# The last output block in two PSUM banks, the wq/wk weights in eight transfers and one cast, and another layout of the bf16 values tile

## The chip, the cores and the metric

The kernel runs on one core of one Trainium2 chip. The metric is the device time of one execution in microseconds (us); smaller is better. The engines are called by the profile's names: PE (TensorE; PEld is its weight load), DVE (VectorE), ACT (ScalarE), POOL (GpSimd), and SP, which issues most of the transfers.

## What is computed

Sigmoid attention over 8 sequences of 448 tokens with 12 heads of 64, followed by a token-mixing MLP. The names are the reference's, cut to what matters:

```python
# q, k, v: (8, 12, 448, 64) float32
scores = q @ k^T / sqrt(64) - log(448)
attn = 1 / (1 + exp(-scores))
x = (attn @ v)                       # laid out as (8, 448, 768)
wq, wk = x @ w_q, x @ w_k            # (768 x 64 weights)
W_tok = wq @ wk^T / sqrt(64)         # (8, 448, 448)
out = relu(W_tok @ x) @ w_out        # (8, 448, 768) float32
```

## The kernel before

**Units of work.** Four heads of one sequence make a quad; there are 24 (three per sequence), numbered 0 to 23. For each quad seven score tiles are computed: `scores` (L298) fills two PSUM banks with four 64x64-tiled matmuls, and ACT turns them into a bf16 tile with one sigmoid over 128x896 (L303). There are 168 of those. `values` (L320) multiplies them with the quad's v and sums over the seven tiles. The MLP of a sequence follows in pieces (`mlp_wqk`, `mlp_tmp`, `mlp_mix`), and the last matrix product goes out in blocks of 384 columns (`out_pair` L509, `out_halves` L549, `out_chunk` L590). The order of all this on the engines is written out by hand: the string `PLAN` has a letter for each step, and the string `BANKS` names the bank or pair of banks that each step takes, in order, of the eight.

**Loads and casts.** Each quad needs q, k and v, 448 KB each in float32. The list `ORDER` gives the order of loading and casting; a name such as k5 is k of quad 5, and w0 stands for the two weight matrices wq and wk together (`load_weights`, L624; later w entries are pieces of wout). It begins:

```python
"W2 q1 k1 k2 q2 v0 k3 q3 v1 q4 k4 v2 w0 k5 q5 w1 v3 v4 .w6 k6 q6 w4 v5 q7 k7 v6 ..."
```

Before it stand q0 and k0, the latter in two parts (L645 to L647). All loads are issued by SP into eight buffers; `pump_loads` issues a load when the entry eight places ahead of it has been cast (`ring[-8] not in cast`), and w0 counts as one entry. The casts to bf16 run on POOL in the order of the list, all but a few that the list marks for DVE: `cast1` for q and k (L192 in one layout, L202 in another) and for v (L202), `cast_now` for w0 (L720). L630 is an issue of wout's load on POOL's own queue, which stands between the casts of q5 and v3.

The program gives the transfers of SP and ACT eight completion semaphores in rotation, and a transfer waits, ahead of its own issue, until the one eight places before it has landed. Counted from the first, q0 is transfer 1, k0 2 and 3, q1 4, k1 5, k2 6, q2 7, v0 8, k3 9, q3 10, v1 11, q4 12, k4 13, v2 14, wq 15, wk 16, k5 17, q5 18.

**wq and wk.** Two transfers put them side by side in one float32 buffer, 128 rows at a time (L624); four POOL casts of 64x384 then write `wqk16` in the order in which the matmuls take the rows, moving half of them to the other 64 partitions (L720).

**The end.** The last sequence pair ends in eight blocks of `out_chunk` on single banks, six 128x128-by-384 matmuls each (L590), in two steps of three. DVE or ACT copies a block to SBUF (L614). The last block is copied by both at once: DVE takes columns 384 to 575 (L611) and ACT columns 576 to 767 (L612). Both read one bank, and the program orders the second reader behind the first. The store (L599) goes in two halves of 64 partitions, one issued by SP and one by ACT.

Of the kernel before, what the change touches and what calls it, by code (L numbers as in the profile page):

```python
# [10 lines left out]
BF16 = mybir.dt.bfloat16  # L11
# [6 lines left out]
def kernel(  # L18
# [29 lines left out]
    def pool(name, bufs, **kw):  # L48
# [4 lines left out]
    p_c16 = pool("c16", 2)  # L53
    p_v16 = pool("v16", 4)
# [24 lines left out]
    )  # L79
    BANKS = BANKS.split()[::-1]  # L80

# [65 lines left out]
    ld = {}  # L147
# [39 lines left out]
    def cast1(n, nm, e):  # L187
        if KIND[n] in "cer" and nm != "v":
            if n not in pq:
                pq[n] = p_c16.tile([P, 2, 2, NI, 32, 2], BF16, tag="qk16", name="qk16")  # L190
            f = pq[n]
            COPY[e](  # L192
                out=f[:, :, "qk".index(nm)].rearrange("p e i d y -> p e y i d"),
                in_=ld.pop((nm, n)).rearrange("p (y i e d) -> p e y i d", y=2, i=NI, e=2),
            )
            ld[nm + "16", n] = f
            if ("q16", n) in ld and ("k16", n) in ld:
                arrange(n, nc.gpsimd)
            return
        p = p_v16 if nm == "v" else p_c16  # L200
        t16 = p.tile([P, NI, 2, HD], BF16, tag=nm + "16", name=nm + "16")
        COPY[e](  # L202
            out=t16.rearrange("p i b d -> p b i d"),
            in_=ld.pop((nm, n)).rearrange("p b (i d) -> p b i d", i=NI),
        )
        ld[nm + "16", n] = t16

    qk = {}
# [104 lines left out]
    def values(n, i, tail, eng):  # L313
        u, j = quads[n]
        if i == 0:
            pv[n] = bank2()
        fb, ps, _ = pv[n]
        for h in range(2):
            for g in range(2):
                nc.tensor.matmul(  # L320
                    ps[HALF[g], h, 0:S], ld["v16", n][HALF[h], i, g, :],
                    ats[n, i][HALF[h], g, :], start=(i == 0), stop=(i == NI - 1),
                )
        if i == NI - 1:
            if tail:
                for h in range(2):
                    read(fb, COPY["vs"[h]](out=xt(u, j)[:, h, 0:S], in_=ps[:, h, 0:S]))
            else:
                read(fb, COPY[eng](out=xt(u, j)[:, :, 0:S], in_=ps[:, :, 0:S]))  # L329
# [158 lines left out]
    chunks = []  # L488
    ot = {}

    opened = []
# [80 lines left out]
    def out_chunk(act, tail):  # L572

        if opened:
            w, m, nb, fb, ps = opened.pop()
            part = 1
        else:
            w, m, nb = chunks.pop(0)
            if nb < 0:
                nb = 0  # L580
                chunks.insert(0, (w, m, 1))
            fb, ps, _ = bank1()
            part = 0
        if nb == 0 and not part:
            ot[0] = p_o.tile([P, D], F32, tag="o", name="o")
        o = ot[0]

        def block(ps, w0, w1, c0, c1):
            for c in range(c0, c1):
                nc.tensor.matmul(  # L590
                    ps, mxs[w][:, 2 * S * c + m * P : 2 * S * c + (m + 1) * P],
                    wout16[:, c, w0:w1], start=(c == 0), stop=(c == NC - 1),
                )

        def store(cols):
            for y in range(2):
                b, i = divmod(2 * m + y, NI)
                eng = nc.scalar if tail and y else nc.sync
                eng.dma_start(  # L599
                    out=out[2 * w + b].rearrange("(p i) d -> p i d", i=NI)[:, i, cols],  # L600
                    in_=o[HALF[y], cols],
                )

        ps = ps[:, 0:NB] if not part else ps
        block(ps, nb * NB, (nb + 1) * NB, part * NC // 2, (part + 1) * NC // 2)
        if not part:
            opened.append((w, m, nb, fb, ps))
            return
        if w == NU // 2 - 1 and not chunks:
            h = NB // 2  # L610
            read(fb, nc.vector.tensor_copy(out=o[:, NB : NB + h], in_=ps[:, 0:h]), keep=True)  # L611
            read(fb, nc.scalar.copy(out=o[:, NB + h :], in_=ps[:, h:]), keep=True)  # L612
        else:
            read(fb, COPY["s" if act else "v"](out=o[:, nb * NB : (nb + 1) * NB], in_=ps), keep=True)  # L614
        split = tail and w == NU // 2 - 1 and m == NI - 1
        if nb or split:
            store(slice(nb * NB, (nb + 1) * NB) if split else slice(0, D))

    w32 = {}

    def load_weights():
        w32["qk"] = p_ld.tile([P, 2 * NI * HD], F32, tag="ld", name="w32")[:, 0:D]
        for x, w in enumerate((moe_w_q, moe_w_k)):
            nc.sync.dma_start(  # L624
                out=w32["qk"].rearrange("p (c n) -> p c n", c=NC)[:, :, 64 * x : 64 * x + 64],
                in_=w.rearrange("(c p) n -> p c n", p=P)
            )

    def load_wout(c):
        nc.gpsimd.dma_start(  # L630
# [11 lines left out]
    def cols(r):  # L642
# [9 lines left out]
        out=ident, in_=ident, compare_op=ALU.not_equal, fill=1.0, base=0,  # L652
# [22 lines left out]
        elif x[0].isupper():  # L675
            BY["s"].append((x[0].lower(), int(x[1:])))
    OTHERS = set(BY["s"] + BY["v"])
    ORDER = [(x[0], int(x[1:])) for x in ORDER.replace(".", "").lower().split()]
    done = dict.fromkeys("SPqkKxWNUMOCgz", 0)
    used, loaded, cast = set(), set(), set()  # L680

# [2 lines left out]
    def pump_loads():  # L684
        while len(loaded) < len(ORDER):
            nm, n = ORDER[len(loaded)]
            if nm == "w" and n:
                loaded.add((nm, n))
                continue
            if len(ring) >= 8 and ring[-8] not in cast:  # L690
                break
            ring.append((nm, n))
            if nm == "w":
                load_weights()
            else:
                load1(n, nm, nc.sync)
            loaded.add((nm, n))
# [13 lines left out]
    def cast_now(nm, n, e):  # L711
        if nm != "w":
            cast1(n, nm, e)
        elif n:
            if n % 3 == 1:
                load_wout(n - 1)
        else:
            for h in range(2):
                for g in range(2):
                    COPY[e](  # L720
                        out=wqk16[HALF[g], h::2],
                        in_=w32["qk"].rearrange("p (c n) -> p c n", c=NC)[HALF[h], g::2],
                    )
        cast.add((nm, n))
        pump_loads()

# [2 lines left out]
    def pump():  # L729
        while pumped[0] < len(ORDER):  # L730
            nm, n = ORDER[pumped[0]]
            if (nm, n) not in OTHERS:
                if not ready(nm, n):
                    break
                cast_now(nm, n, "g")
            pumped[0] += 1

    def cast_next(e):
# [7 lines left out]
    for t16, t32, r, e in ((q016, q0, IA, "v"), (q016, q0, IB, "s"), (k016, k0, KA, "g"), (k016, k0, KB, "g")):  # L746
        COPY[e](
            out=t16[:, r].rearrange("p i b d -> p b i d"),
            in_=t32[:, :, cols(r)].rearrange("p b (i d) -> p b i d", d=HD),
# [119 lines left out]
```

## Time and profile before

| what | us |
|---|---|
| median of 3 runs | 183.09 |
| lowest and highest of them | 182.22, 185.05 |
| the profiled execution, as timed | 182.05 |
| span of its profile | 180.3 |

| engine | busy us | instructions |
|---|---|---|
| PE | 169.6 | 3471 |
| ACT | 160.0 | 212 |
| DVE | 142.1 | 229 |
| POOL | 123.4 | 168 |

The span runs from the first to the last instruction of the profiled execution; what the timed figure has above it (1.8 us) lies around it. Times in the profile's rows count from the span's start. A row of the timeline has the start, the length and, in brackets, the idle time of its engine just before it with what ended that. DMA issues (SPq, ACTq) don't count as busy time of their engine.

### The profile page before, as it was taken

The numbers are of one execution on the slowest core, as the hardware profiler recorded it, in microseconds if no ns is written. First come the engines' busy times: TensorE is split into PE (matmuls) and PEld (weight loads), VectorE is DVE, ScalarE is ACT, GpSimd is POOL, SyncE is SP. The second block draws the span as 40 slices with busy tenths as digits, with TensorE's granted clock in tenths as the row PEclk, the third lists the DMA queues.
The fourth block names the chain that finished last, engine by engine and source line by source line (L and its number), as shares of the span: only waits on it lengthen the run. The fifth ranks groups of instructions, "written<-read, shape, count | busy, mean of one in ns | idle before, by whom it ended". The sixth has DMA issues, their size and how long they took to land.

```text
span 180.3 us, 7970 instructions
## 1 busy us (share of the span) xinstructions
PE 169.6 (94%) x3471; PEld 112.5 (62%) x3472; DVE 142.1 (79%) x229; ACT 160.0 (89%) x212; POOL 123.4 (68%) x168
## 2 busy tenths in 40 slices
PE   7787899889999999999999999999999999999990
PEld 7333555554455445655686768778987789778560
DVE  3239599998989899889899879887999866588810
ACT  4699999999999999999999989999999899985240
POOL 1397799998998999999999999989306990000000
PEclk9999999999999999999999999999999999999998
DMA  5999999999999799989998999983946744442686
GB/s 174 356 394 387 331 382 376 288 302 364 411 340 346 181 306 292 372 285 288 313 282 285 281 374 346 316 266 96 264 118 155 226 95 107 91 91 46 157 241 175
DMA packets 24915, 47.31 MB, mean 262 GB/s; under 512 B 3888, under 2 KB 18480, under 8 KB 24880
## 3 DMA queue, kind: packets, MB, share of 16 engines
q1 hardware_dynamic: 23680, 44.84, 77.0%
q0 software_dynamic: 800, 1.18, 3.6%
q10 hardware_dynamic: 400, 0.79, 1.4%
q8 instruction: 27, 0.44, 1.0%
q14 instruction: 8, 0.07, 0.1%
HBM read 35.78 MB, written 11.01 MB: 260 GB/s over the span
## 4 chain that ended last, share of the span: by engine, by line
PE 67%; DVE 14%; DMA 9%; POOL 4%; SPq 2%; ACT 2%; issue 2%
PE banks L298 13%; PE banks L320 13%; PE banks L590 13%; PE banks L509 11%; DVE qk L232 4%; DMA k<-in_k_dram 4%; DMA v<-in_v_dram 3%; PE banks L549 3%; PE banks L395 3%; DVE xt L329 3%; POOL qk L192 3%; PE banks L358 2%; DVE qk L256 2%; DVE xn L347 1%; DMA out_dram<-o 1%
## 5 line engine op out<-in xcount | busy, mean ns | idle before, releaser
L303 ACT ACTIVATE at<-banks 128x896 bf16<-128x896 f32 x168 | 140.9, 946 | 3.6 <-PE banks L298 2.7
L298 PE MATMUL banks<-qk 64*64 64x448 bf16 x672 | 62.5, 357 | 2.5 <-DVE xt L329 1.4
L320 PE MATMUL banks<-at,v 64*64 64x448 bf16 x672 | 46.5, 350 | 0.1
L298 PEld LDWEIGHTS <-qk 64*64 64x64 bf16 x672 | 25.8, 105 | 21.1 <-issue 12.5
L509 PE MATMUL banks<-wout,mx 64*64 64x384 bf16 x672 | 36.3, 323 | 0.0
L320 PEld LDWEIGHTS <-v 64*64 64x64 bf16 x672 | 23.7, 106 | 6.9 <-issue 0.8
L509 PEld LDWEIGHTS <-mx 64*64 64x64 bf16 x672 | 23.3, 107 | 4.3
L590 PE MATMUL banks<-wout,mx 128*128 128x384 bf16 x132 | 24.8, 327 | 0.0
L192 POOL CAST qk<-q 128x896 bf16<-128x896 f32 x19 | 22.6, 1191 | 0.7 <-DMA q<-in_q_dram 0.2
L450 DVE TENSOR_SCALAR mx<-banks 128x512 bf16<-128x512 f32 (+3 forms) x24 | 21.0, 882 | 2.4 <-PE banks L477 1.6
L161 POOL COPY swap<-qk 32x448 uint32<-32x448 uint32 x28 | 15.8, 564 | 10.2 <-DVE qk L192 8.5
L192 POOL CAST qk<-k 128x896 bf16<-128x896 f32 x18 | 21.5, 1194 | 1.8 <-POOL qk L167 0.9
L329 DVE CAST xt<-banks 128x896 bf16<-128x896 f32 x19 | 20.5, 1081 | 1.4 <-PE banks L320 1.0
L202 POOL CAST v<-v 128x896 bf16<-128x896 f32 x20 | 18.4, 931 | 0.6
L590 PEld LDWEIGHTS <-mx 128*128 128x128 bf16 x132 | 11.9, 98 | 10.7 <-issue 3.9
L164 POOL COPY qk<-qk 32x448 uint32<-32x448 uint32 x28 | 16.6, 592 | 1.6
L263 DVE STREAM_TRANSPOSE qk<-qk 128x448 f32<-128x448 f32 x28 | 17.3, 630 | 0.1
L167 POOL COPY qk<-swap 32x448 uint32<-32x448 uint32 x28 | 15.8, 564 | 1.6
L232 DVE STREAM_TRANSPOSE qk<-qk 32x448 f32<-32x448 f32 x24 | 15.3, 636 | 0.6
L371 DVE COPY xn<-banks 128x1024 bf16<-128x1024 bf16 (+1 forms) x17 | 11.1, 654 | 4.6 <-PE banks L358 4.6
L614 DVE COPY o<-banks 128x384 f32<-128x384 f32 x15 | 8.2, 550 | 1.6 <-PE banks L590 0.8
L358 PEld LDWEIGHTS <-xt 64*64 64x64 bf16 x544 | 7.6, 109 | 1.9 <-issue 1.0
(87 smaller groups left out, 196.2 us busy)
## 6 DMA issues: line engine op xcount, KB each, us to landing
q<-in_q_dram SPq DMA_DIRECT2D x24, 448.0 KB, 7.0
v<-in_v_dram SPq DMA_DIRECT2D x24, 448.0 KB, 6.3
k<-in_k_dram SPq DMA_DIRECT2D x23, 448.0 KB, 7.3
out_dram<-o SPq DMA_DIRECT2D x51, 192.0 KB, 3.5
wout<-in_moe_w_out_dram POOLq DMA_DIRECT2D x2, 576.0 KB, 12.1
wout<-wout SPq DMA_DIRECT2D x12, 96.0 KB, 5.2
out_dram<-o ACTq DMA_DIRECT2D x3, 192.0 KB, 3.4
k<-in_k_dram SPq DMA_DIRECT2D x1, 256.0 KB, 5.2
```

The lines of the kernel that those rows point to most:

```text
L164: eng.tensor_copy(out=w[hi, 0], in_=w[lo, 1])
L192: COPY[e](out=f[:, :, "qk".index(nm)].rearrange("p e i d y -> p e y i d"), in_=ld.pop((nm, n)).rearrange("p (y i e d) -> p e y i d", y=2, ...
L202: COPY[e](out=t16.rearrange("p i b d -> p b i d"), in_=ld.pop((nm, n)).rearrange("p b (i d) -> p b i d", i=NI),)
L232: nc.vector.transpose(out=qk[n][other : other + 32, h].rearrange("p t i n -> p (t i n)").bitcast(F32), in_=w[own : own + 32, 1 - h],)
L263: nc.vector.transpose(out=qk[n][:, t].rearrange("p t i n -> p (t i n)").bitcast(F32), in_=w)
L298: nc.tensor.matmul(sc[HALF[h], g, 0:S], qk[n][HALF[g], h, 1, i, :], qk[n][HALF[g], h, 0].rearrange("p i n -> p (i n)"), start=True, stop=True,
L303: inst = nc.scalar.activation(at, sc[:, :, 0:S], ACTF.Sigmoid, bias=attn_bias, scale=attn_scale)
L320: nc.tensor.matmul(ps[HALF[g], h, 0:S], ld["v16", n][HALF[h], i, g, :], ats[n, i][HALF[h], g, :], start=(i == 0), stop=(i == NI - 1),)
L329: read(fb, COPY[eng](out=xt(u, j)[:, :, 0:S], in_=ps[:, :, 0:S]))
L450: inst = nc.vector.tensor_scalar(dst, ps, moe_scale, 0.0, ALU.mult, ALU.max)
L509: nc.tensor.matmul(ps[HALF[x], y, 0:NB], mx[HALF[y], u, b, 64 * (i - 3 * y) : 64 * (i - 3 * y) + 64], wout16[HALF[y], slot(y, b), x * NB : ...
L590: nc.tensor.matmul(ps, mxs[w][:, 2 * S * c + m * P : 2 * S * c + (m + 1) * P], wout16[:, c, w0:w1], start=(c == 0), stop=(c == NC - 1),)
```

## The change

1. **Last output block.** The three-matmul steps of the block become two blocks of 192 columns, six matmuls each, in two banks. DVE copies the first, ACT the second, and the store follows. The block takes one bank more, so `BANKS` gets one entry more, bank 0. From the 97th entry on the names are exchanged, 0 with 2 and 1 with 3 (01 with 23); no entry is added, removed or moved before the last.
2. **wq and wk.** Eight transfers of 64 partitions and 48 KB each (two matrices, two halves of partitions, two of the interleaved row groups) put the rows straight into the order and the partitions in which they are needed, and one POOL cast of 128x768 takes the place of four of 64x384.
3. **Layout of v.** The bf16 tile of v is [2, 7, 64] per partition instead of [7, 2, 64], so that its cast writes 896 elements in one run instead of runs of 64. The matmuls of `values` read 64 neighbouring elements as before.
4. A mark `*` in `ORDER` would send a v cast to a DMA. `ORDER` has no such mark, so nothing takes that way.

`PLAN` and `ORDER` are not changed.

```diff
-        "45 01 67 45 01 2 3 4 5 6 7 0 1 "
+        "45 23 67 45 23 0 1 4 5 6 7 2 3 0 "
...
-        p = p_v16 if nm == "v" else p_c16
-        t16 = p.tile([P, NI, 2, HD], BF16, tag=nm + "16", name=nm + "16")
+        if nm == "v":
+            t16 = p_v16.tile([P, 2, NI, HD], BF16, tag="v16", name="v16")
...
+                COPY[e](
+                    out=t16.rearrange("p b i d -> p (b i d)"), in_=ld.pop((nm, n)).rearrange("p b x -> p (b x)"),
+                )
+            ld["v16", n] = t16
+            return
+        t16 = p_c16.tile([P, NI, 2, HD], BF16, tag=nm + "16", name=nm + "16")
...
-                    ps[HALF[g], h, 0:S], ld["v16", n][HALF[h], i, g, :],
+                    ps[HALF[g], h, 0:S], ld["v16", n][HALF[h], g, i, :],
...
+        if nb and w == NU // 2 - 1 and not chunks:
+
+            if part:
+                fb, ps, _ = bank1()
+            h = NB // 2
+            c0 = NB + part * h
+            block(ps[:, 0:h], c0, c0 + h, 0, NC)
+            read(fb, COPY["vs"[part]](out=o[:, c0 : c0 + h], in_=ps[:, 0:h]), keep=True)
+            if part:
+                store(slice(NB, D))
+            else:
+                opened.append((w, m, nb, fb, ps))
+            return
...
-        if w == NU // 2 - 1 and not chunks:
-            h = NB // 2
-            read(fb, nc.vector.tensor_copy(out=o[:, NB : NB + h], in_=ps[:, 0:h]), keep=True)
-            read(fb, nc.scalar.copy(out=o[:, NB + h :], in_=ps[:, h:]), keep=True)
-        else:
-            read(fb, COPY["s" if act else "v"](out=o[:, nb * NB : (nb + 1) * NB], in_=ps), keep=True)
+        read(fb, COPY["s" if act else "v"](out=o[:, nb * NB : (nb + 1) * NB], in_=ps), keep=True)
...
         for x, w in enumerate((moe_w_q, moe_w_k)):
-            nc.sync.dma_start(
-                out=w32["qk"].rearrange("p (c n) -> p c n", c=NC)[:, :, 64 * x : 64 * x + 64],
-                in_=w.rearrange("(c p) n -> p c n", p=P)
-            )
+            for g in range(2):
+                for h in range(2):
+                    nc.sync.dma_start(
+                        out=w32["qk"][HALF[g]].rearrange("p (j h n) -> p h j n", j=NJ, h=2)[:, h, :, 64 * x : 64 * x + 64],
+                        in_=w.rearrange("(j g h d) n -> g h d j n", j=NJ, g=2, h=2)[g, h],
+                    )
...
-            for h in range(2):
-                for g in range(2):
-                    COPY[e](
-                        out=wqk16[HALF[g], h::2],
-                        in_=w32["qk"].rearrange("p (c n) -> p c n", c=NC)[HALF[h], g::2],
-                    )
+            COPY[e](out=wqk16.rearrange("p c n -> p (c n)"), in_=w32["qk"])
```

More of the change, by code (lines that the diff above doesn't have):

```diff
@@ L199, in cast1 @@
             return
-        p = p_v16 if nm == "v" else p_c16
-        t16 = p.tile([P, NI, 2, HD], BF16, tag=nm + "16", name=nm + "16")
+        if nm == "v":
+            t16 = p_v16.tile([P, 2, NI, HD], BF16, tag="v16", name="v16")
+            if e == "d":
+                u, j = quads[n]
+                nc.gpsimd.dma_start(
+                    out=t16.rearrange("p b i d -> p b (i d)"),
+                    in_=v[u, 4 * j : 4 * j + 4].rearrange("(g h) (p i) d -> (h p) g (i d)", g=2, i=NI),
+                )
[6 more added lines that the diff above has]
+        t16 = p_c16.tile([P, NI, 2, HD], BF16, tag=nm + "16", name=nm + "16")
         COPY[e](
@@ L602, in store @@
                 )
+        if nb and w == NU // 2 - 1 and not chunks:
[7 more added lines that the diff above has]
+                store(slice(NB, D))
+            else:
+                opened.append((w, m, nb, fb, ps))
+            return
         ps = ps[:, 0:NB] if not part else ps
@@ L623, in load_weights @@
         for x, w in enumerate((moe_w_q, moe_w_k)):
-            nc.sync.dma_start(
-                out=w32["qk"].rearrange("p (c n) -> p c n", c=NC)[:, :, 64 * x : 64 * x + 64],
-                in_=w.rearrange("(c p) n -> p c n", p=P)
-            )
+            for g in range(2):
[3 more added lines that the diff above has]
+                        in_=w.rearrange("(j g h d) n -> g h d j n", j=NJ, g=2, h=2)[g, h],
+                    )
     def load_wout(c):
@@ L677 @@
     OTHERS = set(BY["s"] + BY["v"])
-    ORDER = [(x[0], int(x[1:])) for x in ORDER.replace(".", "").lower().split()]
+    CASTING = {("v", int(x[2:])) for x in ORDER.split() if x[0] == "*"}
+    ORDER = [(x[0], int(x[1:])) for x in ORDER.replace(".", "").replace("*", "").lower().split()]
     done = dict.fromkeys("SPqkKxWNUMOCgz", 0)
@@ L686, in pump_loads @@
             nm, n = ORDER[len(loaded)]
-            if nm == "w" and n:
+            if nm == "w" and n or (nm, n) in CASTING:
                 loaded.add((nm, n))
@@ L734, in pump @@
                     break
-                cast_now(nm, n, "g")
+                cast_now(nm, n, "d" if (nm, n) in CASTING else "g")
             pumped[0] += 1
```

14 rows, old and new, of the table BANKS are left out of this document.

## The prediction

> **What bounds the kernel now.** I read the page first: span, busy shares in slices, chain of waits.
>
> ```profile
> span 180.3 us, 7970 instructions
> ACT  4699999999999999999999989999999899985240
> PE 67%; DVE 14%; DMA 9%; POOL 4%; SPq 2%; ACT 2%; issue 2%
> ```
>
> PE holds most of the chain that ended last, but ACT is full (8 or 9 tenths) from the third slice to the 35th. The timelines of ACT and of the tail say where each rules (start, length, what).
>
> ```profile
> 8.59 51.65 ACT L303 ACTIVATE at<-banks 128x896 bf16<-128x896 f32 x63 [0.38 <-PE banks L298]
> 157.41 0.92 ACT L303 ACTIVATE at<-banks 128x896 bf16<-128x896 f32 x1
> 168.14 7.97 PE L590 MATMUL banks<-wout,mx 128*128 128x384 bf16 x48
> ```
>
> From 8.59 to 60.24 ACT runs 63 sigmoids without a gap, 0.82 us each. In this stage the time is ACT's: work saved on POOL, DVE or SP shortens nothing, and a delay there costs only what is left when the work already ahead of ACT has run out. After the last sigmoid (158.3) PE works off the rest; its last 48 matmuls end at 176.11, and the last copies, the last store and its landing follow in line. So the change has two places: the tail, where every tenth is paid out, and 13 to 30 us, where loads and casts either keep ahead or don't.
>
> **The tail.** The last rows of the same timeline:
>
> ```profile
> 175.38 0.48 ACT L614 COPY o<-banks 128x384 f32<-128x384 f32 x1 [0.70 <-DMA out_dram<-o]
> 175.89 0.50 ACTq L599 DMA_DIRECT2D out_dram<-o  x1
> 176.15 0.36 DVE L611 COPY o<-banks 128x192 f32<-128x192 f32 x1 [4.05 <-PE banks L590]
> 176.54 0.32 ACT L612 COPY o<-banks 128x192 f32<-128x192 f32 x1 [0.69 <-DVE o L611]
> 176.89 0.50 ACTq L599 DMA_DIRECT2D out_dram<-o  x1
> ```
>
> The two copies of the last block run one after the other: DVE to 176.51, then ACT. With a bank each, DVE's copy moves ahead, under the second six matmuls (PE's last 0.5 us hides it). At first sight that frees all that lies between 176.15 and 176.54, 0.39 us. But ACT's own queue has the store of the block before, 175.89 to 176.39. So ACT's copy can start no earlier than 176.39 plus the 0.03 that separates neighbouring rows: 176.42 instead of 176.54. Gain 0.12 us; the store behind it keeps its length and its landing. Bounds: 0.39 if the issue didn't hold ACT's copy, 0 if the second block ends late.
>
> Does it end late? Twelve matmuls of 192 columns take the place of six of 384.
>
> ```profile
> L590 PEld LDWEIGHTS <-mx 128*128 128x128 bf16 x132 | 11.9, 98 | 10.7 <-issue 3.9
> 44.44 0.55 PE banks L342 x8
> L342 PE MATMUL banks<-ident,xt 128*128 128x128 bf16 x56 | 4.3, 220 | 0.1
> ```
>
> Above, 48 matmuls in 7.97 us are 0.166 us each, for 384 columns. A 128x128 weight load lasts 98 ns but lies under the matmul before it: the eight transposes of 128 columns (second row, from the chain), each with such a load, take 0.55 us, and with the 0.22 of the last one off, (0.55 - 0.22) / 7 = 0.047 us apart. So 192 columns go by columns, 0.083 each: 12 x 0.083 = 1.0 us against 6 x 0.166 = 1.0. PE's end stays at 176.11, with 0.31 to spare before 176.42. The other end: if each of the twelve took its load's 98 ns, 1.18 us, the end would be 0.18 later, still inside that 0.31.
>
> A rule of the Trainium skill says otherwise here. The page "TensorE: Matmul & The Clock Gate", section "Part 3: Packing small matmuls", has weight loads overlap running matmuls only where the row groups differ, and its section "LDWEIGHTS" gives 128 columns / 1.2, an estimate of 107 ns. By both, six more loads add 0.64 us in plain sight. The trace disagrees: at 0.166 us for 384 columns there is no room for a load of 98 ns beside each.
>
> **The weights' transfers.** Eight take the place of two, on SP. What SP does around them, and from issue to landing for the transfers at 7.58, 11.98, 13.57 and 14.98 (last column; each asked for alone):
>
> ```profile
> 7.58 0.37 SPq L179 DMA_DIRECT2D q<-in_q_dram  x1
> 11.98 0.38 SPq L179 DMA_DIRECT2D v<-in_v_dram  x1
> 13.14 0.38 SPq L624 DMA_DIRECT2D w<-in_moe_w_q_dram  x1
> 13.57 1.31 SPq L624 DMA_DIRECT2D w<-in_moe_w_k_dram  x1
> 14.98 2.08 SPq L173 DMA_DIRECT2D k<-in_k_dram  x1
> 21.20 0.42 SPq L179 DMA_DIRECT2D v<-in_v_dram  x1
> ...
> q<-in_q_dram SPq DMA_DIRECT2D x1, 448.0 KB, 7.9
> v<-in_v_dram SPq DMA_DIRECT2D x1, 448.0 KB, 8.2
> w<-in_moe_w_k_dram SPq DMA_DIRECT2D x1, 192.0 KB, 8.3
> k<-in_k_dram SPq DMA_DIRECT2D x1, 448.0 KB, 8.0
> ```
>
> q3 (7.58) lands at 15.5, v2 (11.98) at 20.2, wk at 21.9, k5 (14.98) at 23.0. Between q3 and v2 lie v1, q4 and k4, so a load lands every (20.2 - 15.5) / 4 = 1.18 us: the queue is full and its order decides. Both weight matrices take 21.9 - 20.2 = 1.7 us of it.
>
> The SP time itself, 6 x 0.42 = 2.5 us more, would not matter, because SP stands at 14.98 and after it for a full queue (2.08 for one issue). What matters is the rule of the eight semaphores. The weights become transfers 15 to 22; the last of them waits for transfer 14, v2, thus for 20.2, and behind it on SP stand k5, q5, v3, v4, k6, q6, v5. k5 becomes transfer 23 and waits for 15, which follows v2 by about 1.7 / 8 = 0.2 us. So k5 is issued at 20.2 + 0.42 = 20.6 instead of 14.98. No row of before shows a load in the middle of the run that finds an emptying queue; the nearest rows are the load that found it empty, and the loads that found it full.
>
> ```profile
> DMA to landing us min/median/max: 3.3/7.9/8.3
> ```
>
> (q's transfers up to 16 us; 3.3 is q0, the first of all.) By these ends k5 lands at 20.6 + 3.3 = 23.9 or 20.6 + 8.0 = 28.6. I take 23.9, because only the last few weight transfers, 0.2 us each, are still ahead of it. The following loads land 1.18 us apart behind it, as they do now: the stream is 0.9 us late.
>
> **POOL, which hides that.** Its timeline, with PE's first read of v3 (last row) and DVE's first use of k5 and q5 (the row before it):
>
> ```profile
> 22.01 2.18 POOL L720 CAST wqk<-w 64x384 bf16<-64x384 f32 x4 [0.86 <-DMA w<-in_moe_w_k_dram]
> 24.25 1.19 POOL L192 CAST qk<-k 128x896 bf16<-128x896 f32 x1
> 25.34 1.20 POOL L192 CAST qk<-q 128x896 bf16<-128x896 f32 x1
> 26.45 0.89 POOL L630 DMA_DIRECT2D wout<-in_moe_w_out_dram  x1
> 27.34 0.94 POOL L202 CAST v<-v 128x896 bf16<-128x896 f32 x1
> 29.78 1.17 DVE L256 STREAM_TRANSPOSE qk<-qk 128x448 f32<-128x448 f32 x2
> 29.14 0.10 PEld L320 LDWEIGHTS <-v 64*64 64x64 bf16 x1
> ```
>
> ```profile
> L202 POOL CAST v<-v 128x896 bf16<-128x896 f32 x20 | 18.4, 931 | 0.6
> L720 POOL CAST wqk<-w 64x384 bf16<-64x384 f32 x4 | 2.0, 503 | 1.0 <-DMA w<-in_moe_w_k_dram 0.9
> L747 POOL CAST k<-k 128x384 bf16<-128x384 f32 x1 | 0.5, 502 | 3.4 <-DMA k<-in_k_dram 3.4
> L202 DVE CAST v<-v 128x896 bf16<-128x896 f32 x4 | 2.8, 696 | 0.0
> L192 DVE CAST qk<-k 128x896 bf16<-128x896 f32 x2 | 1.4, 698 | 0.0
> ```
>
> A POOL cast costs by its elements: 502 ns for 384, 931 for 896, so 0.84 ns each, and 502 + 384 x 0.84 = 824 ns for the one cast of 768. That is 2.18 - 0.82 = 1.36 us less. The last weight transfer, issued at 20.2, lands at 22.6 if it takes the 2.4 us of the smallest transfers in the trace:
>
> ```profile
> out_dram<-o SPq DMA_DIRECT2D x2, 96.0 KB, 2.4
> ```
>
> The cast then ends at 22.6 + 0.82 = 23.4, and k5's begins when k5 lands, 23.9, against 24.25 now. q5, landing at 25.1, is cast from 25.1, L630 issues from 26.3, v3 is cast from 27.2 to 28.1. Now it is 28.28, and PE reads it at 29.14. The lateness of the loads and the shorter cast cancel, to about 0.1 us, and 0.9 us of cover stays. Without that cover each microsecond later would be one that PE waits.
>
> **The rest** costs nothing. v's longer runs: POOL's 503 ns for runs of 128 and 502 for runs of 64 say that a run's length has no price, and DVE's 696 and 698 that not even scattered elements have. The exchanged bank names keep every distance between two uses, but for two entries at the seam, where the pair free for longer now comes first. Bank 0 was last used eight blocks before.
>
> Sum: -0.12 (between -0.39 and +0.1) in the tail, 0 early: 182.05 - 0.1 = 181.9 against the profiled execution, which lies 0.6% below the median of the runs. The four executions of before have their middle at (182.22 + 183.09) / 2 = 182.65, so I forecast **182.5**.
>
> **The rivals.**
>
> *The loads come too late* (slower). One mechanism: k5, held at the eight semaphores until 20.6, takes the full 8.0 us. It lands at 28.6; k5, q5, L630 and v3 then take 1.19 + 1.20 + 0.89 + 0.94 = 4.2 us, v3 is ready at 32.8, PE waits from 29.14: 3.7 us, and ACT, full before and after, can't win them back: 182.5 + 3.7 = 186.2. It decides from the point where k5 lands after 29.14 - 4.2 = 24.9. For it: seven loads leave SP late at once, and the margin is 1.0 us. Against: they meet a drained queue. On this the Trainium skill has a rule against the change: "SBUF — State Buffer", section "Door 1: The DMA port swizzle", says that 64 partitions reach half the ports (196 against 328 GB/s). Its mechanism in rows of this kernel: the weights would need up to 2 x 1.7 = 3.4 us behind v2, k5 would land no earlier than 20.2 + 3.4 + 1.18 = 24.8, and 0.1 us of margin would be left, the time staying 182.5. No transfer of before has 64 partitions on the SBUF side and stands alone, so the trace doesn't say. It is why I give this rival 0.22 rather than 0.12.
>
> *POOL's time reaches the end* (faster). If 1.36 us less on POOL pulled DVE and then PE forward, 182.5 - 1.4 = 181.1. For: DVE has 14% of the chain, its early part. Against: ACT's 51.65 us without a gap, and the loads' lateness, which eats that time. 0.08.
>
> *The weight loads show* (the change doesn't shorten the tail): by 98 ns each the tail gains 0 to 0.1, by the page's rule it loses 0.64 - 0.31 - 0.12 or about 0.2: 182.6 to 182.8. 0.05.
>
> The forecast keeps 0.65.
>
> **How the numbers follow.** The runs of before lie 1.5% apart, so about 2% (3.7 us) is what a measurement of this kernel can tell from no change. Slower by over 2%: two thirds of the first rival, whose price is just that limit, 0.15, and 0.03 for scatter: 0.18. Faster by over 2%: no case reaches it; 0.04 for scatter. Within: 0.78. The range reaches down to the faster rival, 181.0, and up to 185.9, most of the slower one's way and past the highest run of before.
>
> **What would show it.** In the new profile: L612's place, an ACT copy of 128x192, starting near 176.4 with no DVE before it in brackets, and DVE's copy about 0.5 us earlier; eight L624-type issues about 1.2 us apart, the last at 20.2; k5's issue near 20.6 and landing 3.3 to 4.0 us later; one POOL cast of 128x768 of about 0.82 us; v3 cast before 29.1; ACT without a gap to 60. I am wrong if ACT shows a new gap between 25 and 35 us, if the transfers leave SP at another rhythm, or if the end of ACT's sigmoids moves by more than 0.5 us from 158.3.

## The result, and the profile after

The changed kernel takes 187.68 us (median of four runs, 186.98 to 189.19); the kernel before, beside it on the same chip, 182.86. The ratio is 1.0287, with a 95% interval from 1.0202 to 1.0372; it is that of the means, without the slow run of 185.05 us of the kernel before, which lies over 1.5% above that kernel's fastest. The change makes the kernel slower, and the time lies above the range that was forecast. Its profiled execution took 186.98 us, with a span of 185.2: 4.9 us more than before.

Lines of the page of the changed kernel:

```profile
span 185.2 us, 7990 instructions
ACT  4699998997999999999989997999999989985240
POOL 1498559878899999999999999989405990000000
PE 33%; POOL 29%; DMA 21%; DVE 8%; issue 4%; SPq 2%; ACT 1%; POOLq 0%; ACTq 0%; DVEq 0%
L333 PE MATMUL banks<-at,v 64*64 64x448 bf16 x672 | 46.9, 351 | 1.7 <-POOL v L209 1.3
```

In the chain that ended last POOL went from 4% to 29% and DMA from 9% to 21%. POOL's slices show a hole near the start (a 5 and a 5), and the matmuls of `values` now wait for POOL's casts of v. ACT, which ran from 8.59 to 60.24 without a gap, has gaps in the same stretch:

```profile
8.57 22.02 ACT L316 ACTIVATE at<-banks 128x896 bf16<-128x896 f32 x27 [0.26 <-PE banks L311]
31.27 13.07 ACT L316 ACTIVATE at<-banks 128x896 bf16<-128x896 f32 x16 [0.68 <-PE banks L311]
45.49 17.42 ACT L316 ACTIVATE at<-banks 128x896 bf16<-128x896 f32 x21 [1.16 <-PE banks L311]
...
162.00 0.92 ACT L316 ACTIVATE at<-banks 128x896 bf16<-128x896 f32 x1
```

Its last sigmoid begins at 162.00 instead of 157.41, 4.59 us later. The gaps before 46 make up only 1.84 of it; the rest comes later and is read below. First what starts it. SP's queue, in the timeline (x4 stands for four issues):

```profile
12.89 3.26 SPq L647 DMA_DIRECT2D w<-in_moe_w_q_dram  x4
16.38 4.71 SPq L647 DMA_DIRECT2D w<-in_moe_w_k_dram  x4
21.18 1.27 SPq L173 DMA_DIRECT2D k<-in_k_dram  x1
```

The landings, in the view of DMA issues for 12.8 to 22 us (last column: median us from issue to landing):

```profile
k<-in_k_dram SPq DMA_DIRECT2D x1, 448.0 KB, 4.6
w<-in_moe_w_q_dram SPq DMA_DIRECT2D x4, 48.0 KB, 7.0
w<-in_moe_w_k_dram SPq DMA_DIRECT2D x4, 48.0 KB, 3.6
```

k5 is issued at 21.18 instead of 14.98. A transfer of 48 KB that stands behind full loads takes 7.0 us to land, nearly as long as one of 448 KB did before (8.0), and holds its turn in the rotation of eight semaphores all that time. Each of the last four leaves SP 0.02 us after the landing of the transfer eight places ahead of it; the eighth leaves at 20.49, v2 having landed at 20.47. So once v2 has landed, all that is left in the DMA queue is eight small transfers, 384 KB, where before it was up to eight loads. The windows show the hole that this leaves (length, POOL's busy time, granted clock, DMA share, GB/s). Before:

```profile
20.00:24.00 4.00, 2.89 (x6) 1.00 1.06 381
24.00:40.00 16.00, 15.39 (x20) 1.00 1.08 333
40.00:60.00 20.00, 18.27 (x24) 1.00 0.97 345
```

After:

```profile
20.00:24.00 4.00, 1.44 (x2) 1.00 0.42 81
24.00:40.00 16.00, 12.18 (x14) 1.00 1.06 337
40.00:60.00 20.00, 18.17 (x26) 1.00 1.02 349
```

From 20 to 24 us the DMA engines move 81 GB/s instead of 381; that is (381 - 81) x 4 us = 1.2 MB not moved. POOL does 3.2 us less work from 24 to 40, because it waits for what wasn't moved, and afterwards it works at the same rate as before (18.27 and 18.17 of 20 us): it is late and stays late. POOL's timeline, after:

```profile
23.50 0.83 POOL L742 CAST wqk<-w 128x768 bf16<-128x768 f32 x1 [2.03 <-DMA w<-in_moe_w_k_dram]
25.96 1.19 POOL L192 CAST qk<-k 128x896 bf16<-128x896 f32 x1 [1.63 <-DMA k<-in_k_dram]
...
34.16 0.93 POOL L209 CAST v<-v 128x896 bf16<-128x896 f32 x1 [0.48 <-DMA v<-in_v_dram]
36.09 1.19 POOL L192 CAST qk<-q 128x896 bf16<-128x896 f32 x1 [0.38 <-DMA q<-in_q_dram]
38.29 1.19 POOL L192 CAST qk<-k 128x896 bf16<-128x896 f32 x1 [1.01 <-DMA k<-in_k_dram]
...
124.05 1.20 POOL L192 CAST qk<-k 128x896 bf16<-128x896 f32 x1 [0.59 <-POOL qk L167]
```

and the row of before that answers to the last of these:

```profile
120.05 1.20 POOL L192 CAST qk<-k 128x896 bf16<-128x896 f32 x1 [0.59 <-POOL qk L167]
```

In these rows POOL waits 2.03 + 1.63 + 0.48 + 0.38 + 1.01 = 5.5 us for transfers; before, there was one such wait in the stretch, 0.86 (its row stands in the prediction). The one cast is 2.18 - 0.83 = 1.35 shorter. 5.5 - 0.9 - 1.35 = 3.3 us, most of the 124.05 - 120.05 = 4.0 by which the same cast of a k comes late at the far end of POOL's line. Between 40 us and there POOL has only two waits above 0.15 us in either kernel, 0.52 and 0.30 before, 0.31 and 0.38 after: it has nothing with which to catch up.

ACT follows by steps. Its row of eight sigmoids at 89.13 began at 86.80 before, 2.33 us earlier; a row of nine further on is as late as POOL, 114.78 - 110.77 = 4.01 (timeline, before and after):

```profile
110.77 7.50 ACT L303 ACTIVATE at<-banks 128x896 bf16<-128x896 f32 x9
114.78 7.50 ACT L316 ACTIVATE at<-banks 128x896 bf16<-128x896 f32 x9 [1.19 <-PE banks L311]
```

The chain that ended last says the same. After, it goes over k5 to the transfer of k7, and from 38 to 110 us over POOL's casts and copies, but for two stretches (43 to 54 and 64 to 69 us; start, length, what):

```profile
27.17 11.07 DMA k<-in_k_dram
38.29 1.20 POOL qk L192
...
109.28 1.15 POOL qk L192
110.45 1.17 DVE qk L269 x2
```

Before, it goes mostly over DVE up to 37 us and over PE from there to 103.

### The profile page after: what moved, and what is told of

The parts are those of the page before. It is cut to its first block, busy times and chain, and to the rows that moved or that the text cites. A ratio compares the mean times of both kernels' runs of the same rounds, so it can differ in the third digit from the quotient of the medians.

```text
span 185.2 us, 7990 instructions
## 1 busy us (share of the span) xinstructions
PE 171.0 (92%) x3478; PEld 114.8 (62%) x3478; DVE 142.6 (77%) x229; ACT 160.6 (87%) x212; POOL 122.7 (66%) x165
## 3 DMA queue, kind: packets, MB, share of 16 engines
q0 software_dynamic: 800, 1.18, 3.5%
## 4 chain that ended last, share of the span: by engine, by line
PE 33%; POOL 29%; DMA 21%; DVE 8%; issue 4%; SPq 2%; ACT 1%; POOLq 0%; ACTq 0%; DVEq 0%
DMA k<-in_k_dram 12%; POOL qk L192 12%; PE banks L522 10%; PE banks L333 6%; PE banks L311 5%; DMA v<-in_v_dram 5%; POOL swap L161 4%; POOL qk L167 4%; POOL qk L164 4%; POOL v L209 4%; PE banks L562 3%; PE banks L603 2%; DMA wout<-wout 2%; DVE qk L245 2%; DMA out_dram<-o 1%
## 5 line engine op out<-in xcount | busy, mean ns | idle before, releaser
L333 PEld LDWEIGHTS <-v 64*64 64x64 bf16 x672 | 24.6, 106 | 9.0 <-issue 1.8
L522 PEld LDWEIGHTS <-mx 64*64 64x64 bf16 x672 | 24.0, 107 | 5.0 <-issue 1.3
L603 PE MATMUL banks<-wout,mx 128*128 128x384 bf16 (+1 forms) x138 | 24.8, 320 | 0.1
L276 DVE STREAM_TRANSPOSE qk<-qk 128x448 f32<-128x448 f32 x28 | 17.6, 634 | 3.0 <-POOL qk L164 1.7
L603 PEld LDWEIGHTS <-mx 128*128 128x128 bf16 x138 | 12.4, 98 | 10.5 <-issue 3.9
L269 DVE STREAM_TRANSPOSE qk<-qk 128x448 f32<-128x448 f32 x12 | 7.0, 623 | 2.8 <-POOL qk L192 2.7
```

Of the source, the lines that this page charges most:

```text
L333: nc.tensor.matmul(ps[HALF[g], h, 0:S], ld["v16", n][HALF[h], g, i, :], ats[n, i][HALF[h], g, :], start=(i == 0), stop=(i == NI - 1),)
L522: nc.tensor.matmul(ps[HALF[x], y, 0:NB], mx[HALF[y], u, b, 64 * (i - 3 * y) : 64 * (i - 3 * y) + 64], wout16[HALF[y], slot(y, b), x * NB : ...
L603: nc.tensor.matmul(ps, mxs[w][:, 2 * S * c + m * P : 2 * S * c + (m + 1) * P], wout16[:, c, w0:w1], start=(c == 0), stop=(c == NC - 1),)
```

## The experiments

Three theories stood at the start. S: the turns that small transfers take in the rotation of eight. H: the shape of the transfers, 64 partitions and 48 KB, and what it costs in issue and in ports. R: something in the rest of the change (layout of v, bank names, last block).

The table has for each kernel the transfers that it adds to SP's line, its ratio to the kernel before, and from its profile the DMA rate over the first 28 us, the start of that last cast of POOL's line and the start of the last sigmoid. A dash stands where a kernel's profile is not read here. Each profile is of one execution, and some lie above their kernel's median (wout_early_before 184.8 against 183.17, spread 187.6 against 186.7, half_four 184.34 against 183.53), others below (four_tiny 184.43 against 185.91, six_tiny 186.59 against 187.57); the last three columns are those executions'. In one_cast and four_tiny they hold a stretch of half clock on PE (last section).

| kernel | transfers added | ratio, 95% interval | GB/s, 0 to 28 us | POOL's cast, us | last sigmoid, us |
|---|---|---|---|---|---|
| before | 0 | 1 | 339 | 120.05 | 157.41 |
| the change | 6 | 1.0287 [1.0202, 1.0372] | 286 | 124.05 | 162.00 |
| undo_weights | 0 | 1.0041 [0.9996, 1.0085] | 338 | 120.36 | 157.71 |
| only_weights | 6 | 1.0210 [1.0129, 1.0292] | - | - | - |
| two_tiny | 2 | 1.0068 [1.0041, 1.0094] | 318 | 121.77 | 159.00 |
| half_four | 2 | 1.0106 [1.0060, 1.0151] | 312 | 122.02 | 159.46 |
| four_tiny | 4 | 1.0190 [1.0100, 1.0280] | 315 | 122.08 | 159.32 |
| six_tiny | 6 | 1.0278 [1.0192, 1.0364] | 286 | 124.15 | 161.91 |
| spread | 6 | 1.0250 [1.0208, 1.0291] | 298 | 123.94 | 162.88 |
| one_cast | 0 | 1.0022 [0.9981, 1.0064] | 334 | 121.27 | 158.49 |
| pool_delay | 0 | 1.0261 [1.0187, 1.0335] | 339 | 123.83 | 161.05 |
| wout_early_after | 6 | 1.0242 [1.0196, 1.0287] | 278 | 124.85 | 162.07 |
| wout_early_before | 0 | 1.0024 [0.9990, 1.0058] | 330 | 122.33 | 160.22 |
| soft_weights | -2 | 1.0002 [0.9967, 1.0037] | - | - | - |

**undo_weights**: the changed kernel with the old loading and casting of wq and wk.

```diff
-            for g in range(2):
-                for h in range(2):
-                    nc.sync.dma_start(out=w32["qk"][HALF[g]]..., in_=...[g, h])
+            nc.sync.dma_start(
+                out=w32["qk"].rearrange("p (c n) -> p c n", c=NC)[:, :, 64 * x : 64 * x + 64],
+                in_=w.rearrange("(c p) n -> p c n", p=P)
+            )
...
-            COPY[e](out=wqk16.rearrange("p c n -> p (c n)"), in_=w32["qk"])
+            for h in range(2):
+                for g in range(2):
+                    COPY[e](out=wqk16[HALF[g], h::2], in_=w32["qk"]...[HALF[h], g::2])
```

> The changed kernel with wq and wk as before: two transfers of 128 partitions and four POOL casts; the last block in two banks, the layout of v and the bank names stay changed. Theory S (slots: the eight completion semaphores in rotation hold seven loads back until the eighth weight transfer has left, at 20.5): k5 is issued near 15.0 and lands near 23.0 again, 182.6 us, ratio to before 0.995 to 1.003. Theory H (shape: transfers of 64 partitions and 48 KB are themselves slow to issue and to move): the same, 182.6. Rival R (the rest of the change does it: v's layout or the bank names): 186 to 188, ratio above 1.02.

Measured 1.0041; the interval takes in no change. R falls: what is left of the change, the layout of v, the bank names and the last block, costs at most 0.9%. This kernel has ACT's long row again, from 7.12 to 60.97 us without a gap.

**only_weights**: the kernel before with the eight transfers and the one cast, the same lines the other way round.

> The kernel before with the eight weight transfers and the one cast alone. S and H: the whole loss, 187.5 us, ratio 1.02 to 1.035, k5 issued after 20.5 and landing near 25.8. R: 182.7, ratio 1.00.

Measured 1.0210: that part alone brings the loss.

**six_tiny, four_tiny**: the kernel before, its two weight transfers and four casts kept, with six or four transfers of 8 KB over all 128 partitions behind them, into a tile that nothing reads.

```diff
+    spare = singles.tile([P, 6, 16], F32)
...
+        for s in range(6):
+            nc.sync.dma_start(out=spare[:, s], in_=moe_w_q[128 * s : 128 * s + 128, 0:16])
```

> The kernel before, its two weight transfers and four casts untouched, with six transfers more right behind them on SP: 128 partitions, 64 bytes each, 8 KB a transfer, into a spare tile that nothing reads. They take slots 17 to 22 and move almost no bytes, and none has 64 partitions. S: the last one leaves at about 20.3, k5 (transfer 23) waits for wq's landing at 21.0, and the loads land 2 to 3 us late; 186 to 188.5 us (POOL's casts aren't shortened here). H: six issues of 0.4 us on SP, hidden by the full queue: 182.7 to 183.3.

> The same with four tiny transfers instead of six. S, worked out from the landings of before: the last tiny one waits for q4 (17.7), k5 becomes transfer 21 and waits for k4 (18.9), which is still before the weights have landed (21.9), so the queue doesn't run empty, k5 lands within 0.5 us of 23.0 and the time stays within 1 us of before, 182.7 to 183.7. If every slot taken costs in proportion, two thirds of what six cost: 185 to 186. H: 182.7 to 183.1.

six_tiny moves 48 KB more and loses what the change loses, 1.0278 against 1.0287. None of its added transfers has 64 partitions, so six places in SP's line are enough for the loss, and the shape isn't needed. The hole is the same, too (windows):

```profile
20.00:24.00 4.00, 3.18 (x6) 1.00 0.38 53
```

But what holds k5 there isn't what holds it in the changed kernel (timeline):

```profile
14.88 7.21 SPq L630 DMA_DIRECT2D spare<-in_moe_w_q_dram  x6
22.19 0.38 SPq L174 DMA_DIRECT2D k<-in_k_dram  x1
```

wq, eight places ahead of k5, landed at 21.33, and none of the six had to wait for a landing either. SP stands in the issues themselves, 2.55 us in the first and 1.86 in the second, as it stood in those of k5 and q5 before (2.08 and 1.82): the small transfers take the places of loads at a full queue. In four_tiny and two_tiny it is the same. So these runs show the price of a transfer more in the line; that the semaphores do the holding is read in the changed kernel and in spread, where issues follow such a landing by 0.02 to 0.06 us.

four_tiny contradicts what I expected of it: k5 lands at 24.2, before the 24.9 that the prediction had as the point of decision, and the kernel is 1.9% slower all the same. So the lateness of k5 isn't the measure.

**two_tiny**: the same with two.

> The kernel before, with two transfers of 8 KB (128 partitions, 16 columns of the q weights into a spare tile) behind its two weight transfers: two slots more, none of them with 64 partitions, 16 KB more to move. If a slot costs the same whatever the transfer in it (0.5% or 0.85 us each, from four and six such transfers at 1.019 and 1.028), 183.2 to 184.3, ratio 1.004 to 1.012, beside the 1.0106 that two more transfers of 64 partitions gave. If the 64 partitions made up most of that 1.0106, no change here: 182.0 to 182.9. Issue of k5: near 17, landing 23.4 to 24.

Measured 1.0068, an interval without 1. This is the run that decides the matter, because here the stage that the prediction looked at isn't touched. Its SP queue, in the timeline:

```profile
15.12 4.07 SPq L630 DMA_DIRECT2D spare<-in_moe_w_q_dram  x2
19.29 0.50 SPq L174 DMA_DIRECT2D k<-in_k_dram  x1
```

POOL's line, in the timeline:

```profile
27.45 1.81 POOL L203 CAST v<-v 128x896 bf16<-128x896 f32 x2
...
34.03 1.19 POOL L193 CAST qk<-q 128x896 bf16<-128x896 f32 x1 [0.73 <-DMA q<-in_q_dram]
36.08 1.19 POOL L193 CAST qk<-k 128x896 bf16<-128x896 f32 x1 [0.85 <-DMA k<-in_k_dram]
```

k5 is issued 4.3 us later than before, at 19.29, takes 3.9 us and lands at 23.2 (before 23.0). k5, q5 and v3 are cast when they always were: 24.34 against 24.25, 27.45 against 27.34. The price shows up seven microseconds further on, where POOL waits 0.73 and 0.85 us for q7 and k7, and at the end of POOL's line it is 1.7 us late. The sigmoids, matched one by one with those of before, are 0.3 us late up to 87 us and 1.7 from 112 on: they reach POOL's lateness where they do in the changed kernel. A place given to a small transfer is a load that isn't in flight, and, as I read it, the bytes that weren't moved are missing at whatever load is needed next without reserve.

**half_four**: the kernel before, each weight transfer split into two of 64 partitions; the four casts stay.

```diff
-            nc.sync.dma_start(
-                out=w32["qk"].rearrange("p (c n) -> p c n", c=NC)[:, :, 64 * x : 64 * x + 64], ...)
+            for g in range(2):
+                nc.sync.dma_start(
+                    out=w32["qk"][HALF[g]].rearrange("p (c n) -> p c n", c=NC)[:, :, 64 * x : 64 * x + 64], ...)
```

> The kernel before with its two weight transfers split into four of 64 partitions (rows in the old order, four casts kept). S: k5 becomes transfer 19 and waits for v1 (16.6), where SP stood anyway; k5 lands near 23, the time is 182.5 to 183.5. H: half the ports, k5 lands up to 1.7 us later and the time is 184 or more. A price in proportion to the slots (four_tiny cost 3.5 us for four) would give 184.2.

1.0106 beside 1.0068 for two_tiny, which adds as many transfers with whole partitions; the intervals overlap. If the shape has a price of its own, it is under 1%. In the windows there is a trace of it. half_four:

```profile
16.00:20.00 4.00, 3.06 (x3) 1.00 1.11 283
```

two_tiny:

```profile
16.00:20.00 4.00, 3.67 (x4) 1.00 1.10 323
```

The engines are equally busy (1.11 and 1.10) and move 12% less. The rule of the Trainium skill that the prediction weighed ("SBUF — State Buffer", section "Door 1: The DMA port swizzle", half the ports for 64 partitions) fits that direction, but six_tiny shows that the loss doesn't hang on it.

**spread**: the changed kernel with its eight transfers in two groups of four, one ahead of v2 and one behind k5.

```diff
-"... v1 q4 k4 v2 w0 k5 q5 w1 ..."
+"... v1 q4 k4 x0 v2 k5 w0 q5 w1 ..."
...
+            if nm == "w":
+                load_weights(1)
...
-                load_weights()
+            if nm == "x":
+                load_weights(0)
```

> The changed kernel, all its parts kept, with the same eight transfers of 64 partitions in two groups: wq's four go ahead of v2's load, wk's four behind k5's; the one cast stays behind k5's cast. S: never more than four slots in a row are weights, so the loads around them keep the queue filled: k5 lands near 22.1, q5 near 24.1, v3 near 25.3, as in the kernel before, and the time is 182.0 to 183.5. H (the shape or the count of the transfers costs): 186 to 188, as in the changed kernel.

Measured 1.0250, no better than the change. I had held the row of eight, which empties the queue, for the cause; with the row broken up the hole is shallower and longer (250 GB/s from 20 to 24 us, 286 from 24 to 28) and the loss remains. What counts is how many places are gone, not that they are neighbours.

**pool_delay**: the kernel before with four more POOL casts of 128x768 right behind those of w0, into a tile that nothing reads. No transfer is added.

```diff
+    spare = singles.tile([P, 768], BF16)
...
+            for _ in range(4):
+                COPY[e](out=spare, in_=w32["qk"][:, 0:768])
```

> The kernel before with four casts more on POOL right behind w0's (128x768 into a spare tile that nothing reads), 3.3 us together, no transfer added or moved. If POOL's line of casts has cover as the prediction took it (0.9 us, and ACT's full row behind it), part of it is absorbed: 182.5 + 1 to 2.4. If that line has no cover over the run (it stays late until the end), all of it comes back: 185.5 to 186.5, and ACT's gaps lie at the same quads as in the changed kernel.

3.49 us of POOL work, measured 1.0261, and the last sigmoid 161.05 - 157.41 = 3.64 us later. POOL's line has no cover to speak of; ACT shows at once what PE waits for (timeline):

```profile
32.49 1.73 ACT L304 ACTIVATE at<-banks 128x896 bf16<-128x896 f32 x2 [2.29 <-PE banks L299]
```

**one_cast**: the kernel before with the one cast of 128x768 in place of the four, but with its two transfers. The moving of rows between the partitions is left out.

```diff
-            for h in range(2):
-                for g in range(2):
-                    COPY[e](out=wqk16[HALF[g], h::2], in_=w32["qk"]...[HALF[h], g::2])
+            COPY[e](out=wqk16.rearrange("p c n -> p (c n)"), in_=w32["qk"])
```

> The kernel before with its two weight transfers, and one POOL cast of 128x768 instead of the four of 64x384; the reordering of the weights' rows is left out. No slot is added. If POOL's line has no cover, 1.36 us less on it come off the time: 181.0 to 181.6 (the second rival of the prediction, in its pure form). If ACT bounds the middle: 182.3 to 182.9.

Measured 1.0022: 1.35 us less on POOL bring nothing that can be measured (by the interval at most 0.2%, 0.35 us). In its profile POOL is 0.44 us ahead of before at q7's cast, 32.82 against 33.26, and then waits 0.73 us for k7, for which it doesn't wait before. Together with pool_delay that is an asymmetry. More work on POOL is paid in full, less isn't paid back, since the loads set the pace then.

**wout_early_after, wout_early_before**: in each kernel POOL hands out the first half of the output weights (576 KB as the DMA view counts them; the expectation's third and 1.18 MB are mistaken, for 1.18 MB is what both halves come to in that view) ahead of w0's cast.

```diff
-"... v2 w0 k5 q5 w1 v3 ..."
+"... v2 w1 w0 k5 q5 v3 ..."
```

> The changed kernel with one step moved: POOL hands out the first third of the output weights (1.18 MB, its own queue, outside the rotation of eight) ahead of the weights' cast, near 22.3 instead of 28.4, in the stretch in which the DMA engines stand nearly empty (20 to 24 us). It takes nothing from the rotation, and POOL's 0.89 us for it then lies in a wait. If the loss is the hole itself, bytes that weren't moved and are asked for again later, a large part of the hole (some 1.2 MB short of the kernel before in that stretch) is filled: loads from v5 on at most 3 us late, not 4.6, 183.5 to 185.5. If the loss is that k5, q5 and v3 land late, and the casts behind them, the transfer beside them makes these no earlier: 186.5 to 188.

> The kernel before with the same step moved: here the DMA engines are full from 20 to 28 us, so the 1.18 MB take their share from k5, q5, v3 and v4, which land up to 3 us later than 23.0 to 26.7; POOL's line has 0.9 us of cover there. Hole theory: slower, 183.5 to 186. The other (k5 to v3 late by what the sharing takes, half of it or less): 182.5 to 184.5. Faster than 181 by neither.

1.0242 and 1.0024. POOL issues the transfer at 22.05 in the changed kernel, but the hole stays as it was (97 GB/s from 20 to 24 us): the bytes come only after 24 us, where the queue is full again, and v3 then waits. So this didn't fill the hole, and what filling it would bring remains untried. In the kernel before the move costs nothing that can be measured.

**soft_weights**: the kernel before with its two weight transfers on POOL's own queue, which stands outside the rotation, two transfers on SP fewer than before.

```diff
-            nc.sync.dma_start(
+            nc.gpsimd.dma_start(
```

> The kernel before, with its two weight transfers handed out by POOL on its own queue (as the output weights are) and not by SP: two slots of the rotation fewer than before, the same four casts. POOL issues them near 13 us at some 0.9 each, where its line up to 22 us has 1.7 us of waits that can take them. If the cost of 0.85 us for each slot goes on below two, 181.1 to 181.8. If it doesn't, because ScalarE bounds the first 60 us before as well, 182.2 to 183.0. If POOL's two issues push its casts back beyond the waits, 183 to 185, as the added casts did (3.3 us gave 3.6). The second is taken as likeliest. Wq and wk then must have landed by 22.0, where POOL casts them; the output weights took 11.5 us from issue to landing on that queue, which would be 25.5 and 3.5 us late: in that case up to 187.

Measured 1.0002. Places set free bring nothing here, but the run doesn't show that they can't. In its profile, which the table leaves out (186.47 us, against a median of 183.29), POOL's two issues (0.98 and 0.84 us) stand ahead of its casts, and k5, whose issue waits for a cast, leaves at 16.95, later than before: the free places weren't used. That before the DMA engines are busy all the time already (share 1.04 to 1.14 from 16 to 28 us) speaks against a gain.

## Why the prediction was wrong

**The last block (right).** The prediction had ACT's copy held by the store in ACT's own queue. The rows of the changed kernel:

```profile
179.96 0.48 ACT L635 COPY o<-banks 128x384 f32<-128x384 f32 x1 [0.70 <-DMA out_dram<-o]
180.25 0.36 DVE L624 COPY o<-banks 128x192 f32<-128x192 f32 x1 [3.05 <-PE banks L603]
180.47 0.50 ACTq L612 DMA_DIRECT2D out_dram<-o  x1
181.01 0.32 ACT L624 COPY o<-banks 128x192 f32<-128x192 f32 x1 [0.57 <-PE banks L603]
```

The store lasts to 180.97 and the copy starts 0.04 later. From ACT's copy before to this one it is 1.05 us, where it was 176.54 - 175.38 = 1.16: a gain of 0.11, forecast 0.12. PE's matmuls now end 0.3 us ahead of that copy, as worked out, so the twelve smaller ones hold nothing up. All this is a fortieth of the loss (0.11 of 4.9).

**The issue of k5 (right, 0.6 late).** Forecast 20.6, measured 21.18: v2 landed 0.3 later, and the eighth weight transfer took 0.60 us to issue and not 0.42. The way there, by the rotation of eight, was right.

**The landing of k5 (size wrong).** I took the 3.3 us of the first transfer of all and got 23.9; it took 4.6 and landed at 25.8. With the rival's own sum, 25.8 - 24.9 = 0.9 us late for v3, and ACT's first gap is 0.68. So far the rival that was named for the slower side describes what happened, but it would make the time 183.4 and not 187.

**What the loss is made of (the step that failed).** The prediction says of the loads behind k5 that they "land 1.18 us apart behind it, as they do now: the stream is 0.9 us late", checks that against v3 alone, and leaves it there: "The lateness of the loads and the shorter cast cancel". So the loads' lateness went into the sum as 0. The spacing came out, about 1.2 us, but the lateness was 2.8 to 3.1 us from k5 to q6 and 4.6 at k7 (38.24 against 33.62). And the cover was asked for at v3 only, with the reason "In this stage the time is ACT's". The runs show that several lines are about equally full here: ACT; POOL (15.39 of 16 and 18.27 of 20 us); the DMA engines; and PE, 10.00 of 10 us from 40 to 50. Over the first 28 us the changed kernel moves 286 GB/s where the kernel before moves 339, (339 - 286) x 28 us = 1.48 MB less. At 339 GB/s that is 4.4 us, an estimate, and up to 60 us no stretch has the bandwidth to spare for it (shares of 1.06 and 1.02). POOL, which before has only the two waits of 0.52 and 0.30 us between 22 and 119 us, takes the lateness over (4.0 us), and the sigmoids take most of their 4.59 from POOL, 4.01 of it by 114 us. two_tiny shows it without k5 being late at all; six_tiny without the shape; pool_delay gives POOL a like lateness without any transfer and loses a like amount. In the table the lateness of POOL's cast and that of the last sigmoid go together to within 0.6 us in all kernels but spread.

What isn't shown: that the bytes as such, and not some other effect of fewer transfers in flight, set the 4.4. The experiments changed the number of transfers; none filled the hole. The same estimate, (339 - rate) x 28 us / 339, gives 1.7, 2.2, 2.0, 4.4, 3.4 and 5.0 us for two_tiny, half_four, four_tiny, six_tiny, spread and wout_early_after, and POOL's cast is late by 1.7, 2.0, 2.0, 4.1, 3.9 and 4.8 us in the same executions. wout_early_before falls out of line (0.7 and 2.3). By its ratio four_tiny is slower than half_four, at about the same rate; but the two executions whose rates these are took 184.43 and 184.34 us. By transfers added the cost is 0.3 to 0.5% each (two_tiny 0.34, four_tiny 0.48, six_tiny 0.46).

**The faster rival** (POOL's time reaches the end) falls with one_cast. **The weight loads show** falls with the rows of the last block. **The rest costs nothing** holds to within the interval of undo_weights; the casts of v on POOL take 933 ns, 931 before.

The prediction named what would prove it wrong, a new gap of ACT between 25 and 35 us and an end of the sigmoids moved by more than 0.5 us. Both are there, a gap of 0.68 us at 31.27 and an end 4.59 us later.

## What to carry to other kernels

Where an engine hands out transfers in line, into a full queue or by a fixed number of completion semaphores, count transfers and not bytes: a small one among large ones keeps its place nearly as long as a large one does (7.0 against 8.0 us), and each one is a large load that isn't in flight. Ask of a delayed load not only whether its own reader still gets it in time, but what the DMA engines weren't moving meanwhile, and who further on has no reserve. And before "this engine bounds the stage" excuses a delay on another, look at the slices of all engines and of the DMA: with several lines full, relief of one brought nothing (one_cast), and a delay of POOL or of the loads was paid (pool_delay, two_tiny), some of it 70 us and more further on.

## What the runs showed of the hardware

**PE's clock is halved for 3.4 us, and the wait ahead of it doesn't say when.** In six_tiny PE waits 2.19 us, from 43.4 to 45.6 (timeline):

```profile
45.60 0.38 PE L478 MATMUL banks<-wqk,tmp 64*64 64x448 bf16 x2 [2.19 <-DVE xt L330]
```

The windows behind it (length, PE's busy time, granted clock, DMA share, GB/s); from 47 to 50 the clock is 0.50:

```profile
46.00:47.00 1.00, 1.00 (x10) 0.86 1.01 385
...
50.00:51.00 1.00, 1.00 (x12) 0.93 1.04 401
```

The shares that are missing, 0.14 + 0.50 + 0.50 + 0.50 + 0.07 = 1.71, are 3.4 us at half the clock, and they fall after the wait, on PE's work: ACT has two more gaps there, 0.58 and 0.65 us. pool_delay, spread, four_tiny and one_cast have one such stretch each, as long. A long wait doesn't always bring it: in wout_early_after PE waits 2.77 us, and the clock stays at 1.00 (timeline). And it comes without one: in one_cast PE's longest wait from 12 to 21 us is 0.7 us, the same as in the kernel before, which keeps its clock there (window of one_cast):

```profile
32.09 0.76 PE L333 MATMUL banks<-at,v 64*64 64x448 bf16 x12 [2.77 <-POOL v L209]
20.00:21.00 1.00, 1.00 (x43) 0.50 1.05 346
```

What brings the stretch on stays open. In the profiles of one_cast and four_tiny the sigmoids are 1.0 to 1.1 us late behind it, so it can blur a difference of that size between two executions. The Trainium skill's page "TensorE: Matmul & The Clock Gate", "Part 1: The HAM clock gate", gives a window of about 3.4 us and half the clock after an idle one. The length agrees with the 3.4 us here; an idle time as long stands ahead of none of these five stretches.

**A load into an emptied queue.** 448 KB took 3.6 to 4.6 us from issue to landing (3.6 in six_tiny, 3.9 in two_tiny, 4.3 in four_tiny, 4.6 after the change), against 8.0 in a full queue: so in a full queue about half the time from issue to landing goes to waiting for others.
